# Attention into a weighted network on one core: the low words of the weights placed by GpSimd, halved first pieces, the means in two small products, and a new table of first steps

## The chip, the cores and the metric

One core of a Trainium2 chip runs one program. The metric is device time in microseconds, the median of several runs, from outside the program; a profiled execution also gives the span from the first to the last instruction. The engines are TensorE (PE; its weight loads are PEld), VectorE (DVE), ScalarE (ACT), GpSimd (POOL) and SyncE (SP), whose queue issues nearly all transfers. Each works through its own queue in order, and waits on semaphores for the others.

## The reference, cut to what matters

```
# q, k, v: (4, 8, 768, 64);  w1, w2: (512, 1024);  w3: (1024, 1024);  w_out: (1024, 512)
k_sum = k.reshape(B, H, 24, 32, D).max(axis=3)
v_sum = v.reshape(B, H, 24, 32, D).mean(axis=3)
scores_l = scale * q @ k.T            # only |i - j| < 16 counts
scores_s = scale * q @ k_sum.T + log(32)
a = softmax(concat(masked scores_l, scores_s))
x = a @ concat(v, v_sum)              # then (B * S, H * D) = (3072, 512)
out = ((x @ w1) * (x @ w2)) @ w3 @ w_out
```

`w1`, `w2`, `w3` and `w_out` come as 64-bit floats, as everything else comes as 32-bit floats.

## The kernel before, in words

**Units.** The 3072 tokens are worked in 6 units of 512 tokens. A unit has 4 pairs of heads, and each pair is a step of attention: 16 score products (`sc`), then VectorE's masked minimum (`reduce`) and ScalarE's exponentials (`expose`), GpSimd's small addition on the sums (`invert`, tile `mx`), VectorE's reciprocal, a normalization, 16 transposes (`tp`), two copies out of PSUM (`evacuate`, tile `pt`), 16 products with the values (`po`), and `keep_x`, which keeps x as two words whose sum is exact (a high and a low one). When the 4 pairs of a unit are there, `gate` makes 8 slices f of `(x @ w1) * (x @ w2)`, 24 products each, and `project` multiplies by the folded matrix `wp` and stores.

**Fold.** `w3 @ w_out` is made once, in `fold_weights`: 32 pairs (i, j), each of three products 128x512 (high by high, low by high, high by low). Slices i = 0 and 1 accumulate in PSUM under the tag `mm`, slices 2 and 3 under the tag `tp`, of which there are two banks; the transposes and the `po` of attention use those same two banks. When a slice is complete, `store` copies it to `wp` (ScalarE the high word, VectorE the low one), and frees its bank.

**Weights.** Each 64-bit weight is two 32-bit words. A piece of 512 columns (512 KB) is loaded into a buffer `wraw` of a ring of 10. `convert` turns it into two 32-bit words for TensorE: ScalarE's Prelu rescales the upper words into `wf`; VectorE shifts `wf` left by 3 (line 175) and joins the top 3 bits of the lower words (line 178); ScalarE rounds `wf` to the high word of `w` (line 188); VectorE subtracts for the low word (line 109). In the listings a number after `w` or `wp` tells tiles apart; the first weights are, in order, w_106 and w_115 (w_93 and w_102 after the change) for slices 0 of `w_out` and `w3`; w_253 (w_283) and w_357 (w_385) are slices 2 and 3 of `w_out`, and w_415 (w_448) slice 4 of `w3`.

**Means.** `v_sum` of the first batch is made by TensorE: 6 products of a matrix of constants (`mean_sb`) with rows of v. Those of other batches, and all `k_sum`, are VectorE's reductions.

**Order.** SP's and TensorE's queues are in the order in which the program writes them; the other engines' are put in order by a scheduler. The first part runs in steps t, one for each piece of weights that is worked. `EARLY` is the order of the first pieces, `EARLY_PRODUCTS` that of the fold; `FIRST[s]` is the step in which the scores of pair s are begun, for the first 8 pairs; `LOADS` and `WORK` say which other loads and works go with which piece or step; `RATE` and `LATER_RATE` say how many columns of products TensorE is given in a step; `NORMALIZE` and `SECOND` choose the engine that normalizes a pair, and that makes its second copy out of PSUM. From pair 8 on, two pairs are worked at a time (the last loop of the program), and GpSimd normalizes.

Of the kernel before, what the change touches and what calls it, by code (L numbers as in the profile page):

```python
# [19 lines left out]
P = 128  # L20
# [10 lines left out]
FIRST = (15, 18, 20, 22, 27, 32, 37, 44)  # L31
# [4 lines left out]
    *(("wo", 0, 0), ("w3", 0, 0), ("wo", 0, 1), ("w3", 1, 0), ("wo", 1), ("w3", 2, 0), ("w3", 3, 0)),  # L36
    *(("w3", 0, 1), ("w3", 1, 1), ("wo", 2), ("w3", 2, 1), ("w3", 3, 1), ("wo", 3)),
# [10 lines left out]
NORMALIZE = "VAAAAAAA"  # L48
SECOND = "AAAVAVVA"
SOONER = 400  # L50
RING = 10
# [19 lines left out]
def attention_moe(ctx, tc, qG, kW, kT, vP, vW, vB, mask, w1, w2, w3T, wo, out):  # L71
# [24 lines left out]
    make_identity(nc, ident)  # L96
    mask_sb = const.tile([P, 3, KR], F32, name="mask_sb")


    mean_sb = sb.tile([P, S // P, P], F32, name="mean_sb", tag="v", bufs=2)  # L100
    nc.gpsimd.memset(mean_sb, 0.0)
    for i in range(P // BLOCK):
        for at in (CUT, CUT - 64):
            part = mean_sb.rearrange("p t n -> p (t n)")[i * BLOCK : (i + 1) * BLOCK, at + i :: P + P // BLOCK]
            nc.gpsimd.memset(part[:, : S // P], 1.0 / BLOCK)
# [22 lines left out]
    def weight(name, i, src, shape, part=None):  # L128

        n = src.shape[1] // 2  # L130
        parts = range(n // PIECE) if part is None else [part]
        units.append((name, i, shape, list(parts), len(todo) + len(parts) - 1))
        for k in parts:
            todo.append(src[:, 2 * k * PIECE : 2 * (k + 1) * PIECE])

    def start_loads(at_least):

        while todo or due_loads:
# [8 lines left out]
            nc.sync.dma_start(raw, todo.pop(0))  # L147
# [4 lines left out]
    def convert(name, i, shape, parts, last):  # L152


        n = len(parts) * PIECE
# [6 lines left out]
        for k in range(len(parts)):  # L162
# [3 lines left out]
            low_words.append(words[:, :, 0])  # L166
            nc.scalar.activation(  # L167
                f[:, k * PIECE : (k + 1) * PIECE],
                words[:, :, 1].bitcast(F32),
                AF.Prelu,  # L170
                scale=2.0**-112,
                alpha=-(2.0**32),
            )
            yield
        nc.vector.tensor_scalar(out=bits, in0=bits, scalar1=3, scalar2=None, op0=ALU.logical_shift_left)  # L175
        for k, low_word in enumerate(low_words):
            some = bits[:, k * PIECE : (k + 1) * PIECE]
            nc.vector.scalar_tensor_tensor(  # L178
                out=some, in0=low_word, scalar=29, in1=some, op0=ALU.logical_shift_right, op1=ALU.bitwise_or
            )  # L180
            working.pop(0)
# [4 lines left out]
        at = parts[0] * PIECE  # L186
# [4 lines left out]
        have.update((name, i, part) for part in parts)  # L191

    def fold_weights(order):
        acc = {}
        for i, j in order:
            while not {("w3", i, j * P // PIECE), ("wo", j // 2, j % 2 * DO // PIECE)} <= have:
                yield 0
# [58 lines left out]

    def mean_products(tiles):
        po = ps.tile([P, 512], F32, name="means", tag="sc", bufs=4)
        for i in range(S // P):
            nc.tensor.matmul(  # L260
                po[:KR, :DM],
                lhsT=mean_sb[:, i, :KR],
                rhs=tiles[i // 2][:, i % 2],
                start=i == 0,
                stop=i == S // P - 1,
            )
        return po
# [90 lines left out]
    def normalize_alone(s, sm, mx):  # L358

        if NORMALIZE[s] == "A":  # L360
            for j in range(NI):
                nc.scalar.activation(sm[:, j], sm[:, j], AF.Copy, scale=mx[:, 2, j : j + 1])
        else:
            nc.vector.tensor_tensor(sm, sm, mx[:, 2].unsqueeze(2).broadcast_to([P, NI, KR]), ALU.mult)

    def transposes(sm):

        tp = [ps.tile([P, 512], F32, name="tp", bufs=2) for _ in range(2)]
# [43 lines left out]
    def gate(f, x, hs):  # L412
        acc = []
        for w in range(2):
# [6 lines left out]
            for c in range(NC):  # L421
                while (GATES[w], k, c * FQ // PIECE) not in have:
                    yield 0
# [45 lines left out]
    def queue(name, i, part=None):  # L469
        src, shape = {"wo": (wo, (2, DO)), "w3": (w3T, (NJ, P)), "w1": (w1, (NC, FQ)), "w2": (w2, (NC, FQ))}[name]  # L470
        weight(name, i, src[i], shape, part)
# [118 lines left out]
    def means():  # L590
        po = mean_products(vraws)
        vraws.clear()
        vs[0] = sb.tile([KR, DM], F32, name="vs0", tag="pt", bufs=6)
        nc.scalar.copy(vs[0], po[:KR, :DM])

    LOADS = {
        7: [lambda: nc.sync.dma_start(mask_sb, mask)],
        8: [lambda: rows(1)],
        11: [lambda: fetch(0)],
        12: [lambda: keys(1)],  # L600
        13: [lambda: keys(0)],
        14: [lambda: rows(0)],
        15: [lambda: rows(2), lambda: fetch_values(0)],
        16: [lambda: fetch(1)],
        18: [lambda: keys(3)],
        21: [lambda: fetch(2), lambda: fetch_values(1)],
        22: [lambda: keys(2)],
        24: [lambda: fetch(3)],
        25: [lambda: fetch_values(2)],
        28: [lambda: fetch_values(3)],  # L610
# [3 lines left out]
        14: [means, lambda: summaries(0, 1, kraws.pop(1)), lambda: fill(1)],  # L614
        19: [lambda: fetch_sums(0)],
        20: [lambda: load_second(0), lambda: load_second(3), lambda: summaries(0, 2, kraws.pop(2)), lambda: fill(2)],
        21: [lambda: load_second(1), lambda: summaries(0, 3, kraws.pop(3)), lambda: fill(3), lambda: fetch_sums(1)],
# [159 lines left out]
```

## Time and profile before

| what | value |
| --- | --- |
| time, median of 3 runs | 543.22 us (542.31 to 544.02) |
| the profiled execution: time; its span | 541.49 us; 539.7 us |
| mean granted TensorE clock | 0.993 |
| PE busy; PEld busy | 517.6 us (96%); 419.9 us (78%) |
| DVE; ACT; POOL busy | 238.6 us; 239.8 us; 56.8 us |
| read from HBM; written | 58.51 MB; 6.29 MB |

A line of a timeline gives the start and the length in us of a row of like instructions, engine, line, operation and tiles, the shapes, and how many; in brackets the idle time of the engine ahead of them and what ended it. A line of windows gives for a stretch its length, then the busy time of PE, PEld, DVE, ACT and POOL with numbers of instructions, the granted clock, the busy share of the transfer engines, and GB/s. A line of groups ends with busy time, mean ns of one, and idle time ahead. Matmuls of 32-bit words that aren't rounded are recorded as two.

### The profile page before, as it was taken

The page shows a single profiled execution, that of the slowest core. Times are in us where ns is not written, and L with a number is a line of the kernel's source. Part 1 is how long each engine was busy: PE and PEld are TensorE (multiplying, and loading weights), DVE is VectorE, ACT ScalarE, POOL GpSimd, SP SyncE. Part 2 cuts the span into 40 slices and gives each one's busy share as a digit, 9 for nine tenths or more (in the row PEclk, how much of TensorE's full clock was granted, in tenths as well). Part 3 has the DMA queues.
Part 4 walks back from the last instruction along what each step waited for, and adds up shares of the span by engine and source line. Part 5 has one row for each costly group of instructions (what it writes and reads, how often), then busy time and mean ns, then how long its engine had stood idle before and what let it go on. Part 6 is the DMA issues. An engine that isn't in the chain of part 4 may idle for free.

```text
span 539.7 us, 9919 instructions
## 1 busy us (share of the span) xinstructions
PE 517.6 (96%) x3852; PEld 419.9 (78%) x3852; DVE 238.6 (44%) x686; ACT 239.8 (44%) x688; POOL 56.8 (11%) x103
## 2 busy tenths in 40 slices
PE   2897999999999999999999999999999999899997
PEld 1655777888788888888888888888888888788885
DVE  5879889998504227633253043251142350222210
ACT  5548998876436127126254153261172361222210
POOL 1010221110003001103002011021020020000000
PEclk9997999999999999999999999999999999999999
DMA  8999699775614005642050150050150020000001
GB/s 305 406 371 342 193 306 350 244 210 169 205 57 152 0 24 146 202 142 80 0 149 21 60 170 21 0 166 23 60 170 1 16 60 39 21 21 0 1 19 58
DMA packets 30574, 67.21 MB, mean 125 GB/s; under 512 B 4032, under 2 KB 7616, under 8 KB 30528
## 3 DMA queue, kind: packets, MB, share of 16 engines
q1 hardware_dynamic: 27072, 60.30, 34.7%
q10 hardware_dynamic: 3456, 6.29, 3.1%
q8 instruction: 30, 0.49, 0.4%
q14 instruction: 16, 0.13, 0.1%
HBM read 58.51 MB, written 6.29 MB: 120 GB/s over the span
## 4 chain that ended last, share of the span: by engine, by line
PE 91%; DVE 3%; ACT 3%; DMA 1%; issue 1%; POOL 0%; SPq 0%; POOLq 0%; ACTq 0%
PE mm L113 79%; PE po L393 5%; PE sc L319 4%; PE tp L373 3%; DVE w L109 1%; DMA wraw<-in_w3T_dram 1%; DVE wf L178 1%; ACT w L188 1%; PE means L260 1%; ACT sm L347 1%; DVE wf L175 1%; ACT wf L167 0%; ACT pt L378 0%; ACT wp L211 0%; DVE wp L109 0%
## 5 line engine op out<-in xcount | busy, mean ns | idle before, releaser
L113 PE MATMUL mm<-x,w 128*128 128x512 f32 x1152 | 265.1, 390 | 0.0
L113 PEld LDWEIGHTS mm<-x,w 128*128 128x128 f32 x1152 | 215.4, 188 | 45.8 <-issue 0.5
L113 PE MATMUL mm<-wp,h 128*128 128x512 f32 x576 | 134.1, 391 | 0.0
L113 PEld LDWEIGHTS mm<-wp,h 128*128 128x128 f32 x576 | 107.5, 188 | 22.8 <-issue 0.2
L347 ACT ACTIVATE sm<-sm,mx 128x120 f32<-128x120 f32 x192 | 73.7, 386 | 17.4 <-DVE mx L333 16.4
L438 DVE TENSOR_TENSOR g<-mm,g 128x512 f32<-128x512 f32 x48 | 33.1, 690 | 93.2 <-PE mm L113 90.8
L439 ACT CAST h<-g 128x512 fp32r<-128x512 f32 x48 | 29.6, 617 | 90.4 <-DVE g L438 90.4
L113 PE MATMUL mm<-w,w 128*128 128x512 f32 x192 | 52.4, 424 | 12.4 <-ACT w L188 11.4
L113 PEld LDWEIGHTS mm<-w,w 128*128 128x128 f32 x192 | 37.0, 200 | 24.9 <-ACT w L188 13.3
L457 ACT COPY o<-mm 128x512 f32<-128x512 f32 x24 | 14.0, 584 | 81.4 <-PE mm L113 81.4
L382 DVE COPY pt<-tp 120x512 f32<-120x512 f32 x19 | 13.1, 690 | 75.6 <-PE tp L373 75.6
L109 DVE TENSOR_TENSOR h<-g,h 128x512 fp32r<-128x512 f32 x48 | 35.7, 744 | 24.1 <-ACT h L439 23.9
L435 ACT COPY g<-mm 128x512 f32<-128x512 f32 x48 | 28.0, 584 | 35.9 <-PE mm L113 35.9
L333 DVE CUSTOM_DVE_ANT_0 sm<-sc,mask_sb 128x120 f32<-128x120 f32 x192 | 40.9, 275 | 3.9 <-PE sc L319 3.9
L347 ACT ACTIVATION_READ_ACCUMULATOR sm<-sm,mx 128x1 f32 x192 | 36.4, 189 | 0.0
L306 POOL COPY k<-ks 128x96 f32<-128x96 f32 (+1 forms) x32 | 10.2, 331 | 248.1 <-DMA k<-in_kW_dram 207.4
L109 DVE TENSOR_TENSOR x<-po,x 128x512 fp32r<-128x512 f32 x24 | 16.6, 690 | 36.0 <-ACT x L404 36.0
L356 POOL TENSOR_TENSOR sm<-sm,mx 128x960 f32<-128x960 f32 x16 | 29.1, 1820 | 6.0 <-DVE mx L353 5.0
L167 ACT ACTIVATE wf<-wraw 128x512 f32<-128x512 f32 x40 | 26.2, 673 | 6.3 <-DMA wraw<-in_wo_dram 2.8
L393 PEld LDWEIGHTS po<-pt,v 120*64 120x64 f32 x768 | 23.7, 138 | 5.1 <-issue 2.5
L378 ACT COPY pt<-tp 120x512 f32<-120x512 f32 x24 | 14.0, 583 | 30.7 <-PE tp L373 30.7
L188 ACT CAST w<-wf 128x1024 fp32r<-128x1024 f32 (+1 forms) x25 | 21.9, 877 | 12.7 <-DVE wf L178 12.6
(33 smaller groups left out, 295.1 us busy)
## 6 DMA issues: line engine op xcount, KB each, us to landing
k<-in_kW_dram SPq DMA_DIRECT2D x24, 368.0 KB
wraw<-in_w3T_dram SPq DMA_DIRECT2D x16, 512.0 KB
wraw<-in_w_dram SPq DMA_DIRECT2D x16, 512.0 KB
q<-in_qG_dram SPq DMA_DIRECT2D x24, 256.0 KB
raw<-in_kT_dram SPq DMA_DIRECT2D x16, 384.0 KB
out_dram<-o ACTq DMA_DIRECT2D x24, 256.0 KB
v<-in_vW_dram SPq DMA_DIRECT2D x24, 192.0 KB
raw<-in_vB_dram SPq DMA_DIRECT2D x12, 384.0 KB
```

The costliest lines, as they stand in the source:

```text
L109: eng.tensor_tensor(dst, src, hi.bitcast(F32), ALU.subtract)
L113: nc.tensor.matmul(acc, lhsT=a, rhs=b, start=first and i == 0, stop=last and i == len(terms) - 1)
L167: nc.scalar.activation(f[:, k * PIECE : (k + 1) * PIECE], words[:, :, 1].bitcast(F32), AF.Prelu, scale=2.0**-112, alpha=-(2.0**32),)
L188: nc.scalar.copy(hi, f)
L319: nc.tensor.matmul(sc[h][64 * g : 64 * g + 64, i * KR : (i + 1) * KR], lhsT=q[rows, i * P + 64 * g : i * P + 64 * g + 64], rhs=k[rows, i, ...
L333: nc.vector.tensor_tensor_reduce(out=sm[:, j], in0=sc[h][:, i * KR : (i + 1) * KR], in1=mask_sb[:, 0 if blk == 0 else 2 if blk == BLOCKS - ...
L347: nc.scalar.activation(sm[:, j], sm[:, j], AF.Exp, bias=mx[:, 0, j : j + 1], scale=-1.0, accum_out=mx[:, 1, j : j + 1])
L356: nc.gpsimd.tensor_tensor(sm, sm, mx[:, 2].unsqueeze(2).broadcast_to([P, NI, KR]), ALU.mult)
L393: nc.tensor.matmul(po[cols, at : at + 64], lhsT=v[:, g, i, cols], rhs=pt[g][:, (h * NBLK + i) * 64 : (h * NBLK + i + 1) * 64], start=True, ...
L435: nc.scalar.copy(g, a[:, :U])
L438: nc.vector.tensor_tensor(g, acc[1][:, :U], g, ALU.mult)
L439: nc.scalar.copy(h[:, 0], g)
```

## The change

GpSimd takes the lower words of a piece in its `wraw` buffer, multiplies them by 2^-29 and clips at 7, which leaves their top 3 bits as a number; VectorE then shifts `wf` and joins both in one operation, where it took two. The first four pieces have 256 columns (slice 0 of `w_out` and of `w3`, by halves). The means are made with 24 columns: 24 products of 24x128, of which four write side by side in 32 partitions each, four copies out of PSUM, 4 products that spread the result over the wanted rows, and one copy; GpSimd makes the two matrices of constants in step 3 (`CONSTANTS`), the second by 8 copies of the identity. Normalization of pairs 1, 3 and 5 goes from ScalarE to VectorE (that of pair 0 was there), the second copies of pairs 3, 5 and 6 go from VectorE to ScalarE, and that of pair 4 from ScalarE to VectorE. The steps and the tables are new. In the last loop, when nothing is left to begin, the second pair's transposes use two banks of the tag `sc`.

```
-FIRST = (15, 18, 20, 22, 27, 32, 37, 44)
+FIRST = (18, 20, 22, 25, 31, 38, 42, 45)
...
-    *(("wo", 0, 0), ("w3", 0, 0), ("wo", 0, 1), ("w3", 1, 0), ("wo", 1), ("w3", 2, 0), ("w3", 3, 0)),
-    *(("w3", 0, 1), ("w3", 1, 1), ("wo", 2), ("w3", 2, 1), ("w3", 3, 1), ("wo", 3)),
+    *(("wo", 0, 0, 256), ("w3", 0, 0, 256), ("wo", 0, 256, 256), ("w3", 0, 256, 256), ("wo", 0, 512)),
+    *(("w3", 1, 0), ("wo", 1), ("w3", 2, 0), ("w3", 3, 0), ("w3", 0, 512), ("w3", 1, 512), ("wo", 2)),
+    *(("w3", 2, 512), ("w3", 3, 512), ("wo", 3)),
...
-NORMALIZE = "VAAAAAAA"
-SECOND = "AAAVAVVA"
+NORMALIZE = "VVAVAVAA"
+SECOND = "AAAAVAAA"
...
+            nc.gpsimd.tensor_scalar(
+                out=words[:, :, 0], in0=words[:, :, 0], scalar1=2.0**-29, scalar2=7.0, op0=ALU.mult, op1=ALU.min
+            )
             yield
-        nc.vector.tensor_scalar(out=bits, in0=bits, scalar1=3, scalar2=None, op0=ALU.logical_shift_left)
-        for k, low_word in enumerate(low_words):
-            some = bits[:, k * PIECE : (k + 1) * PIECE]
+        for (k, length), low_word in zip(parts, low_words):
+            some = bits[:, k - at : k - at + length]
             nc.vector.scalar_tensor_tensor(
-                out=some, in0=low_word, scalar=29, in1=some, op0=ALU.logical_shift_right, op1=ALU.bitwise_or
+                out=some, in0=some, scalar=3, in1=low_word, op0=ALU.logical_shift_left, op1=ALU.bitwise_or
             )
...
     def mean_products(tiles):
         po = ps.tile([P, 512], F32, name="means", tag="sc", bufs=4)
         for i in range(S // P):
-            nc.tensor.matmul(
-                po[:KR, :DM],
-                lhsT=mean_sb[:, i, :KR],
-                rhs=tiles[i // 2][:, i % 2],
...
+            for p in range(NPAIR):
+                nc.tensor.matmul(
+                    po[32 * p : 32 * p + NB, :P],
+                    lhsT=constants["means"][:, i],
+                    rhs=tiles[i // 2][:, i % 2, p * P : (p + 1) * P],
...
+        means = sb.tile([P, P], F32, name="means_sb", tag="pt", bufs=6)
+        nc.vector.memset(means, 0.0)
+        for p in range(NPAIR):
+            nc.scalar.copy(means[32 * p : 32 * p + NB], po[32 * p : 32 * p + NB, :P])
+        yield
+        po = ps.tile([P, 512], F32, name="means", tag="sc", bufs=4)
+        for p in range(NPAIR):
+            nc.tensor.matmul(po[:KR, p * P : (p + 1) * P], lhsT=constants["spread"][:, p, :KR], rhs=means, start=True, stop=True)
+        vs[0] = sb.tile([KR, DM], F32, name="vs0", tag="pt", bufs=6)
+        nc.scalar.copy(vs[0], po[:KR, :DM])
...
-        15: [lambda: rows(2), lambda: fetch_values(0)],
+        17: [lambda: rows(2)],
...
-    RATE = 6600
-    LATER_RATE = 6944
+    RATE = 5600
+    LATER_RATE = 8944
...
-                        pts.append(evacuate(transposes(sms.pop(last[k])[0])))
+                        spare = {} if now or k == 0 else {"tag": "sc", "bufs": 4}
+                        pts.append(evacuate(transposes(sms.pop(last[k])[0], **spare)))
```

How the order moves, in three places. In each listing a row is an instruction of one engine's queue (line, operation, tiles, shape), with a count where it stands several times.

At the start of ScalarE's queue: the Prelu of the first pieces and the casts to the high words. Before, with pieces of 512 columns:

```order
L167 ACTIVATE wf<-wraw 128x512 x2
L188 CAST w_106<-wf 128x512
L167 ACTIVATE wf<-wraw 128x512
L188 CAST w_115<-wf 128x512
L167 ACTIVATE wf<-wraw 128x512
L188 CAST w_106<-wf 128x512
```

The same start after the change:

```order
L163 ACTIVATE wf<-wraw 128x256 x4
L163 ACTIVATE wf<-wraw 128x512
L185 CAST w_93<-wf 128x256
L185 CAST w_102<-wf 128x256
L185 CAST w_93<-wf 128x256
L163 ACTIVATE wf<-wraw 128x512 x2
L185 CAST w_102<-wf 128x256
```

The first cast stood behind two pieces of 512 columns; it now stands behind four of 256 and one of 512.

In TensorE's queue, from the scores of pair 0 to the products `po` of pair 0 (w_357 and w_385 are the last slice of `w_out` in the fold's first part). Before:

```order
L319 MATMUL sc<-k,q 64x120 x16
L113 MATMUL mm<-w_357,w_115 128x512 x6
L113 MATMUL mm<-w_357,w_137 128x512 x6
L113 MATMUL mm<-w_357,w_171 128x512 x6
L113 MATMUL mm<-w_357,w_196 128x512 x6
L373 MATMUL tp<-ident,sm 120x64 x16
L319 MATMUL sc<-k,q 64x120 x16
L113 MATMUL mm<-w_106,w_415 128x512 x6
L113 MATMUL mm<-w_162,w_415 128x512 x6
L113 MATMUL mm<-w_253,w_415 128x512 x3
L393 MATMUL po<-pt,v 64x64 x16
```

And after:

```order
L347 MATMUL sc<-k,q 64x120 x16
L106 MATMUL mm<-w_385,w_102 128x512 x6
L106 MATMUL mm<-w_385,w_157 128x512 x6
L106 MATMUL mm<-w_385,w_196 128x512 x6
L106 MATMUL mm<-w_385,w_218 128x512 x6
L347 MATMUL sc<-k,q 64x120 x16
L106 MATMUL mm<-w_93,w_448 128x512 x6
L106 MATMUL mm<-w_185,w_448 128x512 x6
L402 MATMUL tp<-ident,sm 120x64 x16
L106 MATMUL mm<-w_283,w_448 128x512 x6
L106 MATMUL mm<-w_385,w_448 128x512 x6
L422 MATMUL po<-pt,v 64x64 x16
```

The transposes of pair 0 stood right behind the fold's first part; now the scores of pair 1 and 12 products of slice 4 stand between.

In GpSimd's queue, from the first means to the first additions on `mx`. Before:

```order
L306 COPY k<-ks 128x4x24
L294 COPY v<-vs_314 24x512 x4
L306 COPY k<-ks 128x4x24
L352 TENSOR_SCALAR mx<-mx 128x8 x2
L294 COPY v<-vs_314 24x512 x2
```

And after:

```order
L170 TENSOR_SCALAR wraw<-wraw 128x512 x5
L334 COPY k<-ks 128x4x24
L322 COPY v<-vs_367 24x512 x2
L170 TENSOR_SCALAR wraw<-wraw 128x512
L322 COPY v<-vs_367 24x512 x2
L170 TENSOR_SCALAR wraw<-wraw 128x512 x5
L380 TENSOR_SCALAR mx<-mx 128x8
L334 COPY k<-ks 128x4x24
L380 TENSOR_SCALAR mx<-mx 128x8
```

The addition on pair 0's `mx` stood behind copies alone; it now stands behind the lower words of five more pieces of weights.

More of the change, by code (lines that the diff above doesn't have):

```diff
@@ L126, in attention_moe, with weight @@
     begun, due_loads, kraws, vraws = [0], [], {}, {}
-    def weight(name, i, src, shape, part=None):
+    def weight(name, i, src, shape, at=None, length=PIECE):
         n = src.shape[1] // 2
[L131 to L134, printed above, removed]
+        parts = [(k, PIECE) for k in range(0, n, PIECE)] if at is None else [(at, length)]
+        units.append((name, i, shape, parts, len(todo) + len(parts) - 1))
+        for k, length in parts:
+            todo.append(src[:, 2 * k : 2 * (k + length)])
     def start_loads(at_least):
@@ L158, in convert @@
         low_words = []
-        for k in range(len(parts)):
+        for k, length in parts:
             raw = loading.pop(0)
@@ L190, in convert @@
         low(nc.vector, lo, f, hi)
-        have.update((name, i, part) for part in parts)
+        have.update((name, i, c) for c in range(at, at + n, P))
     def fold_weights(order):
@@ L195, in fold_weights @@
         for i, j in order:
-            while not {("w3", i, j * P // PIECE), ("wo", j // 2, j % 2 * DO // PIECE)} <= have:
+            while not {("w3", i, j * P), *(("wo", j // 2, j % 2 * DO + c) for c in range(0, DO, P))} <= have:
                 yield 0
@@ L421, in gate @@
             for c in range(NC):
[L422 removed]
+                while (GATES[w], k, c * FQ) not in have:
                     yield 0
```

128 lines of the change are left out of this document (70 added, 58 removed).

## The prediction

> **What bounds the kernel now.** I read the page's busy times first, then windows cut at the places where TensorE's work changes.
>
> ```profile
> span 539.7 us, 9919 instructions
> PE 517.6 (96%) x3852; PEld 419.9 (78%) x3852; DVE 238.6 (44%) x686; ACT 239.8 (44%) x688; POOL 56.8 (11%) x103
> ```
>
> ```profile
> 0.00:9.50 9.50, 0.00 (x0) 0.00 (x0) 2.94 (x6) 4.33 (x6) 1.85 (x15) 1.00 0.77 263
> 9.50:17.75 8.25, 7.27 (x15) 3.79 (x15) 7.98 (x14) 6.03 (x10) 0.00 (x0) 1.00 1.03 404
> 17.75:28.44 10.69, 8.74 (x36) 6.59 (x36) 8.70 (x15) 5.54 (x9) 0.00 (x0) 1.00 1.02 405
> 28.44:45.57 17.13, 17.13 (x90) 11.50 (x90) 12.94 (x33) 10.38 (x29) 3.66 (x6) 1.00 1.04 379
> 45.57:52.55 6.98, 3.20 (x49) 2.59 (x49) 6.53 (x10) 5.37 (x9) 0.23 (x1) 0.64 1.04 325
> 52.55:87.00 34.45, 33.54 (x372) 26.26 (x368) 30.65 (x87) 30.76 (x97) 6.55 (x14) 0.97 0.84 273
> 87.00:463.70 376.70, 376.70 (x2909) 310.41 (x2905) 155.02 (x506) 162.50 (x506) 44.52 (x67) 1.00 0.32 100
> 463.70:468.60 4.90, 3.51 (x98) 3.20 (x97) 1.68 (x3) 1.75 (x3) 0.00 (x0) 1.00 0.01 3
> ```
>
> From 87 to 463.7 us TensorE, the first busy figure, is never idle. What can be won lies before 87, in the 1.4 us idle at 463.7 to 468.6, and in the means. Up to 45.57 the transfer engines are full (share 1.02 to 1.04, about 405 GB/s, so 1.29 us for a piece of 512 KB); VectorE, the third figure, is nearly full from 9.5 to 17.75 and from 45.57 to 87. The worst stretch is 45.57 to 52.55, where the granted clock is 0.64. TensorE's timeline:
>
> ```profile
> 28.44 3.95 PE L113 MATMUL mm<-w,w 128*128 128x512 f32 x16 [0.53 <-DVE w L109]
> 32.23 5.31 PE L260 MATMUL means<-rows,mean_sb 128*120 128x512 f32 x12
> 38.85 1.05 PE L319 MATMUL sc<-k,q 64*64 64x120 f32 x32
> 39.84 5.73 PE L113 MATMUL mm<-w,w 128*128 128x512 f32 x24
> 47.97 0.36 PE L373 MATMUL tp<-ident,sm 64*120 64x64 f32 x1 [2.41 <-DVE wp L109]
> 49.70 1.11 PE L373 MATMUL tp<-ident,sm 64*120 64x64 f32 x15 [1.37 <-DVE wp L109]
> 52.55 4.54 PE L113 MATMUL mm<-w,w 128*128 128x512 f32 x15
> ```
>
> A fold product costs 0.24 us (5.73 over 24). Pair 0's transposes wait twice for VectorE to free the `tp` banks, and the 15 products behind them run at 0.30 us each. What VectorE does meanwhile:
>
> ```profile
> 46.16 1.16 DVE L364 TENSOR_TENSOR sm<-sm,mx 128x960 f32<-128x960 f32 x1
> 47.83 1.22 DVE L109 TENSOR_TENSOR w<-wf,w 128x1024 fp32r<-128x1024 f32 x1
> 48.97 0.68 DVE L109 TENSOR_TENSOR wp<-mm,wp 128x512 fp32r<-128x512 f32 x1
> ```
>
> **The change part by part.** Prices by shape:
>
> ```profile
> L178 DVE SCALAR_TENSOR_TENSOR wf<-wraw,wf 128x512 uint32<-128x512 uint32 x40 | 26.6, 690 | 0.5
> L167 ACT ACTIVATE wf<-wraw 128x512 f32<-128x512 f32 x40 | 26.2, 673 | 6.3 <-DMA wraw<-in_wo_dram 2.8 <-DMA wraw<-in_w3T_dram 1.8 <-DMA wraw<-in_w_dram 1.5
> L188 ACT CAST w<-wf 128x1024 fp32r<-128x1024 f32 x15 | 15.7, 1050 | 5.9 <-DVE wf L178 5.7
> L175 DVE TENSOR_SCALAR wf<-wf 128x1024 uint32<-128x1024 uint32 x15 | 10.3, 689 | 0.4 <-ACT wf L167 0.4
> ```
>
> *Lower words.* VectorE loses one operation of 0.69 us for each 1024 columns. GpSimd gains one of 512 for each piece, beside ScalarE's Prelu (0.67). No row has that operation; GpSimd's nearest rows, and VectorE's beside them:
>
> ```profile
> 38.29 0.99 POOL L294 COPY v<-vs 24x512 f32<-24x512 f32 x1 [5.54 <-ACT vs L594]
> 39.32 0.61 POOL L294 COPY v<-vs 24x512 f32<-24x512 f32 x1
> 94.57 1.30 DVE L109 TENSOR_TENSOR w<-wf,w 128x1024 fp32r<-128x1024 f32 x1
> 94.85 1.28 POOL L294 COPY v<-vs 24x256 f32<-24x256 f32 x1
> 95.79 0.88 DVE L109 TENSOR_TENSOR h<-g,h 128x512 fp32r<-128x512 f32 x1
> 217.31 1.79 POOL L356 TENSOR_TENSOR sm<-sm,mx 128x960 f32<-128x960 f32 x1 [1.02 <-DVE vs L248]
> 217.80 1.84 DVE L109 TENSOR_TENSOR h<-g,h 128x512 fp32r<-128x512 f32 x1 [0.45 <-ACT h L439]
> ```
>
> A copy of 512 takes 0.61, and the operation with two inputs 1.79 for 960, so 0.95 for 512: the new one lies between, under the 1.29 in which a piece lands, and GpSimd keeps up. But the two engines hold each other. The copy at 94.85 ends behind VectorE's subtraction (95.87), and the next subtraction takes 0.88 where 0.69 is usual; the one at 217.80 waits for GpSimd's end and takes 1.84. So a lower word can cost VectorE nothing (it falls beside a reduction or an operation on PSUM), 0.4 (twice the 0.2 of a copy of 256), 0.62 (the 1.15 of the last row, by columns), or its whole 0.95. I take 0.3, that is 0.4 in three cases of four; the ends stay for the range.
>
> The Trainium skill (SBUF — State Buffer, section Who interferes with whom) says that a VectorE instruction with two SBUF inputs and a GpSimd instruction that reads SBUF exclude each other for a whole instruction, whoever comes first. By that rule the join and the low-word subtraction, which both have two, would wait out 0.61 to 0.95 wherever GpSimd is first, and the sum would be the second rival's. The trace agrees in kind (1.84 at 217.80), but has no row for the new operation.
>
> *First pieces.* The fifth load ends at the same number of bytes as the third did. ScalarE's first cast now stands behind that load's Prelu, and the first product needs three casts of 256, so it comes at about 9.8 instead of 9.5. That is hidden by the next wait, the second half of `w_out`'s slice 2. Loads are in order, and one landing is seen here:
>
> ```profile
> 13.56 0.70 ACT L167 ACTIVATE wf<-wraw 128x512 f32<-128x512 f32 x1 [0.30 <-DMA wraw<-in_w3T_dram]
> ```
>
> That is the 7th unit of 512 KB. The half slice stands at 13.35 units before (12 pieces, one of rows, the mask) and at 14.85 after (two key loads more): 21.7 and 13.5 + 7.85 x 1.29 = 23.6 us. Behind it come Prelu, join, cast and subtraction, 0.67 + 0.69 + 1.05 + 1.22 = 3.6: the products go on at 27.2, where VectorE's backlog held them until 28.44.
>
> *Means.* 12 half-rate records of 512 columns take 5.3 us; the 32 of 120 columns at 38.85 take 1.05, a third of what their columns would take in turn, so products in separate columns of the array do run side by side. I take 1.4 for the 24 and 0.9 for the four (bounds: 2.2 and 6.2 in all). But the third load of rows stands at 22.8 units (22.1 before): 13.5 + 15.8 x 1.29 = 33.9, while TensorE is there at 27.2 + 18 x 0.24 = 31.5. The last 8 products end at 34.4; the four copies wait behind the cast of w_385 and take about 1.5; then 0.9: 36.9, against 37.5. So 3 us less work brings 0.6.
>
> *The stretch at 45.57.* Its 6.98 us hold 1.7 of work at full clock (tp 0.68, sc 1.05), and the 15 slow products lose another 1.0: 6.3 lost. The first part of the fold now ends at 45.0; scores of pair 1 and 12 products (3.9) cover until 48.9. Pair 0's transposes want the normalization and slice 3's low word. ScalarE's exponentials stand behind the Prelu of the piece at 27 units, 28.4 + 8.4 x 1.38 (at 379 GB/s) = 40.0; with 8 exponentials, three casts to `wp`, one of w_448 and a Prelu between (3.1 + 1.7 + 1.1 + 1.3) they end at 47.2. GpSimd's addition also stands behind a piece at 31 units, 46 us. Then reciprocal 0.2, normalization 1.16, `wp` 0.68, with semaphores 50 to 51. I take 50.7 (ends 48.9 and 52): 1.8 of waiting, and 0.5 for w_448's low word. 6.3 - 2.3 = 4.0 won. From there to the gate the waits for ScalarE's copies (about 2, two with only 12 products ahead) are as long as the 0.9 idle and the smaller ones of before: 0, within 1.
>
> So the gate could begin 0.6 + 4.0 = 4.6 earlier, at 82.4. *Whether its weights are there* is VectorE's matter:
>
> ```profile
> 49.00:101.00 52.00, 50.38 (x479) 40.03 (x481) 47.68 (x126) 45.48 (x136) 9.32 (x20) 0.95 0.90 294
> 99.76 1.21 DVE L109 TENSOR_TENSOR w<-wf,w 128x1024 fp32r<-128x1024 f32 x1
> 102.44 0.74 PE L113 MATMUL mm<-x,w 128*128 128x512 f32 x2
> ```
>
> The second slice of w2 is ready at 101.0 and used at 102.4: nearly no slack, with VectorE 47.7 of 52 us busy since the end of w_415 (49.05). In the same stretch after: 8 shifts fall away (-5.5), three normalizations come (+3.5), a join, a second copy and some `wp` and gate work shift (-1.4): 44.3, plus 14 lower words at 0.3 = 4.2, plus half of the 4.3 idle: 50.7. From w_448's end at 46 that is 96.7. TensorE wants it at 82.4 + 60 x 0.23 = 96.2. Given back: 0.5, and as much again for ScalarE, nearly as busy (45.5): 1.0. Later weights stand further ahead of their use in the new order.
>
> *Tail.*
>
> ```profile
> 463.68 0.68 PE L373 MATMUL tp<-ident,sm 64*120 64x64 f32 x16
> 465.13 0.73 PE L373 MATMUL tp<-ident,sm 64*120 64x64 f32 x16 [0.76 <-ACT pt L378]
> 466.49 2.09 PE L393 MATMUL po<-pt,v 120*64 120x64 f32 x64 [0.62 <-ACT pt L378]
> ```
>
> With banks of their own the second transposes follow at once: 0.76 + 0.62, less 0.3 that the copies still need: 1.1.
>
> The sum: 4.6 - 1.0 + 1.1 = 4.7 off the profiled execution's 541.49 us (span 539.7 and 1.8 around it). That execution lies 1.7 under the median of 543.22; off the median it is 538.5.
>
> **The rivals.** *All of it shows*: lower words fall beside other work, pair 0 isn't late (1.8 less), the gate isn't either (1.0), and the small waits before it shrink by 1.5: 543.2 - 9.0 = 534.2. For it: VectorE is 4.3 us idle in that window; against: two engines there are over 87% busy.
>
> *GpSimd holds VectorE* (slower): each lower word costs 0.95. Then w2's slice is ready at 96.7 + 14 x 0.65 = 105.8, 9.6 late; 4.6 and 1.1 are won: 543.2 + 9.6 - 5.7 = 547.1. It decides from 0.62 a word on (101.2, 5.0 late, which with ScalarE's share eats the rest). For it: 1.84 at 217.80; against: 0.88 at 95.79.
>
> *The conversions take it all back*: VectorE's idle stays as it is and 0.45 a word is lost, or the four products of the means run in turn (3.9 more): 543, no change.
>
> **How the numbers follow.** About 0.3% (1.6 us) is what a measurement of this kernel can tell from no change. The forecast (536.5 to 541.5) gets 0.47, all of it showing 0.25, no change 0.15, slower 0.13. Faster is 0.47 + 0.25. The forecast's own range is 536.5 to 541.5; with the rivals, leaving a tenth out on each side, 533.5 to 544.8.
>
> **What would show it.** Right: no wait over 2.5 us on TensorE between 40 and 60, the clock at 1.0 there; the joins of VectorE at about 0.69 with few over 0.9; gate from 82 to 84; the two rows of transposes at the end without a gap. Wrong: joins with a mean over 0.95, GpSimd's new operation near 1 us and TensorE waiting on `w` behind the gate's start; a TensorE wait of over 4 us at the means.

## The result and the profile after

The changed kernel takes 565.38 us (median, 564.52 to 566.64) against 542.76 for the kernel before beside it: ratio 1.0415, interval 1.0391 to 1.044. It is 22.6 us slower where 4.7 us less were forecast, and far outside the range. The profiled execution has a span of 562.9 us. Its page, the line of busy times:

```profile
span 562.9 us, 10063 instructions
...
PE 521.7 (93%) x3896; PEld 422.5 (75%) x3896; DVE 232.0 (41%) x667; ACT 236.0 (42%) x674; POOL 152.2 (27%) x149
```

TensorE and VectorE work about as long as before; GpSimd has gone from 56.8 to 152.2 us. Two groups by shape (busy time, mean ns of one, then the idle time ahead of them and what ended it):

```profile
L170 POOL TENSOR_SCALAR wraw<-wraw 128x512 uint32<-128x512 uint32 x38 | 84.9, 2233 | 10.4 <-DMA wraw<-in_w_dram 6.5 <-DMA v<-in_vW_dram 1.3
...
L176 DVE SCALAR_TENSOR_TENSOR wf<-wf,wraw 128x512 uint32<-128x512 uint32 x38 | 26.7, 707 | 26.3 <-POOL wraw L170 25.8 <-DMA wraw<-in_w3T_dram 0.5
```

One lower word of 512 columns takes GpSimd 2.23 us, where the prediction had at most 0.95. The join on VectorE takes 0.71 us as forecast, but VectorE sat idle 25.8 us for GpSimd ahead of joins. The timelines of GpSimd and of VectorE show the queue:

```profile
14.54 21.18 POOL L170 TENSOR_SCALAR wraw<-wraw 128x512 uint32<-128x512 uint32 x9
36.66 12.31 POOL L170 TENSOR_SCALAR wraw<-wraw 128x512 uint32<-128x512 uint32 x5
```

```profile
21.69 0.69 DVE L176 SCALAR_TENSOR_TENSOR wf<-wf,wraw 128x512 uint32<-128x512 uint32 x1 [0.83 <-POOL wraw L170]
24.26 0.69 DVE L176 SCALAR_TENSOR_TENSOR wf<-wf,wraw 128x512 uint32<-128x512 uint32 x1 [1.88 <-POOL wraw L170]
26.82 0.69 DVE L176 SCALAR_TENSOR_TENSOR wf<-wf,wraw 128x512 uint32<-128x512 uint32 x1 [1.86 <-POOL wraw L170]
```

Nine words in a row without a gap, 21.18 / 9 = 2.35 us each. The joins follow at GpSimd's pace, 2.57 us from one to the next (24.26 - 21.69, 26.82 - 24.26), while a piece needs 1.29 us to land at the rate before the change. From 14.5 us on, GpSimd is a queue that falls behind. It holds up the loads too, since a buffer is free only when its join is done: SP's loads of weights (line 142) waited 15.9 us for joins in all, against 3.1 before (line 147). On TensorE:

```profile
11.76 1.65 PE L106 MATMUL mm<-w,w 128*128 128x512 f32 x3 [11.76 <-ACT w L185]
...
29.14 14.28 PE L106 MATMUL mm<-w,w 128*128 128x512 f32 x52 [4.41 <-DVE w L102]
43.35 1.51 PE L279 MATMUL means<-rows,picks 128*24 128x128 f32 x48
49.31 2.03 PE L293 MATMUL means<-means_sb,picks 128*120 128x128 f32 x8 [4.44 <-ACT means_sb L289]
...
69.97 0.36 PE L402 MATMUL tp<-ident,sm 64*120 64x64 f32 x1 [5.23 <-DVE sm L393]
...
103.35 0.34 PE L422 MATMUL po<-pt,v 120*64 120x64 f32 x4 [1.71 <-ACT pt L407]
...
104.80 2.79 PE L106 MATMUL mm<-x,w 128*128 128x512 f32 x11
```

Before, the row that begins with the fold's 15th record, as the one at 29.14 does here, was:

```profile
17.75 8.01 PE L113 MATMUL mm<-w,w 128*128 128x512 f32 x34 [0.37 <-DVE w L109]
```

The first product is at 11.76 instead of 9.52. The fold's 15th record is at 29.14 instead of 17.75; from there the 52 records up to the means run without a wait, and the means begin at 43.35 instead of 32.23. Their four last products wait 4.44, pair 0's transposes 5.23, and the gate begins at 104.80 instead of 87.00. That is 17.8 of the 23.2 us by which the span grew. The windows (after the length comes TensorE's busy time; the granted clock is third from the end) show the rest:

```profile
0.00:104.80 104.80, 71.70 (x600) 54.01 (x600) 64.16 (x146) 60.11 (x150) 82.10 (x72) 0.93 0.78 262
104.80:486.00 381.20, 377.00 (x2899) 308.32 (x2896) 154.10 (x502) 161.08 (x500) 70.10 (x78) 1.00 0.33 100
```

33 us of the first 104.8 are idle, at a mean clock of 0.93. Behind the gate 4.2 us are idle (381.20 - 377.00) where before had none. The tail came out as forecast, 32 transposes in one row and 0.20 of waiting where there were 0.76 and 0.62:

```profile
488.10 1.16 PE L402 MATMUL tp<-ident,sm 64*120 64x64 f32 x32
489.46 2.19 PE L422 MATMUL po<-pt,v 120*64 120x64 f32 x64 [0.20 <-ACT pt L407]
```

### The profile page after: what moved, and what is told of

The parts are those of the page before. It is cut to its first block, busy times and chain, and to the rows that moved or that the text cites. A ratio compares the mean times of both kernels' runs of the same rounds, so it can differ in the third digit from the quotient of the medians.

```text
span 562.9 us, 10063 instructions
## 1 busy us (share of the span) xinstructions
PE 521.7 (93%) x3896; PEld 422.5 (75%) x3896; DVE 232.0 (41%) x667; ACT 236.0 (42%) x674; POOL 152.2 (27%) x149
## 4 chain that ended last, share of the span: by engine, by line
PE 74%; POOL 4%; DMA 3%; DVE 3%; ACT 2%; issue 1%; POOLq 0%
PE mm L106 65%; PE po L422 3%; POOL wraw L170 3%; PE sc L347 3%; PE tp L402 2%; DMA raw<-in_kT_dram 2%; DMA wraw<-in_w_dram 2%; ACT sm L375 1%; DVE vs L244 1%; DVE w L102 1%; ACT sm L390 0%; POOL k L334 0%; DVE ks L227 0%; DVE h L102 0%; DVE wf L176 0%
## 5 line engine op out<-in xcount | busy, mean ns | idle before, releaser
L170 POOL TENSOR_SCALAR wraw<-wraw 128x512 uint32<-128x512 uint32 (+1 forms) x42 | 89.7, 2136 | 14.1 <-DMA wraw<-in_w_dram 6.5
L106 PE MATMUL mm<-w,w 128*128 128x512 f32 x192 | 56.2, 448 | 21.3 <-ACT w L185 12.6
L106 PEld LDWEIGHTS mm<-w,w 128*128 128x128 f32 x192 | 40.0, 216 | 34.0 <-ACT w L185 14.0
L334 POOL COPY k<-ks 128x96 f32<-128x96 f32 (+1 forms) x32 | 11.7, 379 | 194.8 <-DMA k<-in_kW_dram 186.4
L464 ACT COPY g<-mm 128x512 f32<-128x512 f32 x48 | 28.0, 584 | 33.9 <-PE mm L106 33.9
L411 DVE COPY pt<-tp 120x512 f32<-120x512 f32 x17 | 11.6, 690 | 74.1 <-PE tp L402 74.1
L176 DVE SCALAR_TENSOR_TENSOR wf<-wf,wraw 128x512 uint32<-128x512 uint32 (+1 forms) x42 | 28.4, 680 | 33.4 <-POOL wraw L170 32.9
L185 ACT CAST w<-wf 128x1024 fp32r<-128x1024 f32 (+2 forms) x27 | 22.0, 824 | 28.6 <-DVE wf L176 28.5
L380 POOL TENSOR_SCALAR mx<-mx 128x8 f32<-128x8 f32 x24 | 6.2, 259 | 96.7 <-ACT sm L375 96.2
L163 ACT ACTIVATE wf<-wraw 128x512 f32<-128x512 f32 (+1 forms) x42 | 26.3, 645 | 11.2 <-DMA wraw<-in_wo_dram 5.5
L102 DVE TENSOR_TENSOR w<-wf,w 128x1024 fp32r<-128x1024 f32 (+2 forms) x27 | 28.1, 1046 | 6.5 <-ACT w L185 6.5
```

The lines of the kernel that those rows point to most:

```text
L102: eng.tensor_tensor(dst, src, hi.bitcast(F32), ALU.subtract)
L106: nc.tensor.matmul(acc, lhsT=a, rhs=b, start=first and i == 0, stop=last and i == len(terms) - 1)
L163: nc.scalar.activation(f[:, k : k + length], words[:, :, 1].bitcast(F32), AF.Prelu, scale=2.0**-112, alpha=-(2.0**32),)
L170: nc.gpsimd.tensor_scalar(out=words[:, :, 0], in0=words[:, :, 0], scalar1=2.0**-29, scalar2=7.0, op0=ALU.mult, op1=ALU.min)
L176: nc.vector.scalar_tensor_tensor(out=some, in0=some, scalar=3, in1=low_word, op0=ALU.logical_shift_left, op1=ALU.bitwise_or)
L185: nc.scalar.copy(hi, f)
```

## The experiments

Ratios are to the kernel before, run on the same chip; one per cent is 5.4 us. Four theories were to be told apart: GpSimd's operation is slow by itself; VectorE holds it (or is held); the new order and the other edits cost as well; VectorE's work ahead of the gate sets the time.

**The price of the operation (price).** GpSimd tries forms on a scratch tile behind the last attention step:

```
for t in (apart, together, apart as float32, together as float32):
    tensor_scalar(t, t, 2**-29, 7.0, mult, min)   # line 692
    tensor_scalar(t, t, 2**-29, mult)             # line 693
    tensor_copy(t, t)                             # line 694
```

> The kernel before, with GpSimd trying operations of 128x512 on a scratch tile behind the last attention step, where VectorE is about 15% busy; three of each: two operations (mult, min), one (mult), a plain copy; on uint32 and on float32; with words 8 bytes apart and side by side. Theory 'the operation itself is slow': the uint32 operation with words 8 bytes apart takes 1.9 to 2.1 us here too, as its shortest in the changed kernel (1.97), and some of the other forms are far shorter (a float copy 0.6). Rival 'VectorE holds it': with VectorE nearly idle it takes 0.6 to 0.95.

Measured, GpSimd's groups by shape (mean ns of one at the end):

```profile
L692 POOL TENSOR_SCALAR trial<-trial 128x512 f32<-128x512 f32 x6 | 12.0, 2005 | 0.5
L692 POOL TENSOR_SCALAR trial<-trial 128x512 uint32<-128x512 uint32 x6 | 11.7, 1955 | 0.5
L693 POOL TENSOR_SCALAR trial<-trial 128x512 uint32<-128x512 uint32 x6 | 9.1, 1523 | 0.5
L693 POOL TENSOR_SCALAR trial<-trial 128x512 f32<-128x512 f32 x6 | 9.1, 1522 | 0.5
L694 POOL COPY trial<-trial 128x512 f32<-128x512 f32 x6 | 4.1, 682 | 0.4
L694 POOL COPY trial<-trial 128x512 uint32<-128x512 uint32 x6 | 3.7, 623 | 0.4
```

The operation takes 1.96 us beside a VectorE that is busy for 13.63 of the 53 us from 470 to 523. Neither the type nor the distance of the words matters: uint32 and float32 differ by 0.05 on average (one of the float32 words took 2.30), and one by one, words 8 bytes apart take 1.97 to 1.99 (that one apart, which ran beside a subtraction of VectorE), side by side 1.92 or 1.93. What counts is what is done to a word: nothing 0.62 to 0.68, one operation 1.52, two 1.96 to 2.01. So the copies that the prediction took as the lower bound say little of arithmetic. The theory holds; "VectorE holds it" is left with 0.27 of the 2.23. Only the profile of this kernel's one run (543.71 us) is used.

**The words taken back (words_back), alone (words_alone), every second one (words_half).**

```
- gpsimd.tensor_scalar(low, low, 2**-29, 7.0, mult, min)         # words_back
+ vector.tensor_scalar(bits, bits, 3, logical_shift_left)
- vector.scalar_tensor_tensor(some, some, 3, low, shift_left, or)
+ vector.scalar_tensor_tensor(some, low, 29, some, shift_right, or)
```

words_alone is the reverse of these lines in the kernel before; words_half has them for every second piece.

> The changed kernel with the lower words taken back from GpSimd: VectorE shifts the upper word and joins the lower one in two operations, as before; all else as changed. Theory 'GpSimd's 2.1 us a word is the whole loss': the rest of the change is worth what the prediction said or less, 536 to 543 us, the gate begins at 82 to 87 us, no wait of TensorE at the means over 2 us. Rival 'the new order costs as well' (loads of the second batch, means, first steps): over 548.

> The kernel before with the one edit alone: GpSimd places the lower words (40 pieces of 512), VectorE joins in one operation. Theory 'GpSimd's 2.1 us a word is the whole loss': 40 x 2.1 = 84 us of GpSimd's time ahead of the last weight, so the gate begins about 20 us late as in the changed kernel: 560 to 572 us. Rival 'the new order costs as well': 545 to 555.

> The changed kernel with every second piece's lower word on GpSimd, the other on VectorE in two operations. GpSimd then has 21 words x 2.1 = 44 us, one per two landed pieces (2.6 us and more). Theory 'GpSimd is slow but a queue that keeps up costs nothing': 537 to 544, within 3 us of the kernel with all words taken back. Rival 'a word on GpSimd is late by its 2.1 us each time, since VectorE's join waits for it': half of the loss stays, 548 to 556.

Measured: words_back 546.94 us, ratio 1.0098 (1.0071 to 1.0125); words_alone 562.19, 1.0375 (1.0355 to 1.0395); words_half 548.41, 1.0123 (1.0096 to 1.015). GpSimd's words alone cost 20 us in the old order and 17 in the new one. Half of them cost 1 to 2 us more than none, which the intervals cannot tell from nothing; VectorE still waited 11.6 us for GpSimd there. That is within the 3 us that the theory allowed, though the time lies in the rival's range (548 to 556), since words_back itself came out higher than expected. words_back lies between its theory (536 to 543) and its rival (over 548): with the lower words as before, the rest of the change loses 5 us. TensorE in it:

```profile
10.59 1.65 PE L106 MATMUL mm<-w,w 128*128 128x512 f32 x3 [10.59 <-ACT w L183]
...
32.02 3.98 PE L106 MATMUL mm<-w,w 128*128 128x512 f32 x16 [0.53 <-DVE w L102]
54.01 0.69 PE L400 MATMUL tp<-ident,sm 64*120 64x64 f32 x16 [2.16 <-DVE sm L391]
88.67 0.34 PE L420 MATMUL po<-pt,v 120*64 120x64 f32 x4 [2.99 <-ACT pt L405]
```

The gate begins at 90.85 instead of 87.00. So 3.9 of the 4.3 us by which this execution's span (544.0) is longer lie ahead of the gate; as the tail wins 1.1, some 1.5 more are lost behind it.

**One operation instead of two (one_op).**

```
- gpsimd.tensor_scalar(low, low, 2**-29, 7.0, mult, min)
+ gpsimd.tensor_scalar(low, low, 7.49 * 2**-32, mult)
```

> The changed kernel with GpSimd's operation cut to one multiplication by 7.49 x 2^-32, which rounds to 0 to 7 without the minimum (the lowest bits of the weights differ a little). Theory 'GpSimd's time per word is the loss': a word of 512 takes 1.52 instead of 1.95, so 42 words some 17 us less of GpSimd's time; the loss against the kernel with the words taken back (18 us) shrinks by more than half: 549 to 556 us. Rival 'it is the hand-over from GpSimd to VectorE, whatever its length': 560 or more.

Measured: 555.62 us, ratio 1.0257 (1.0239 to 1.0276).

```profile
L170 POOL TENSOR_SCALAR wraw<-wraw 128x512 uint32<-128x512 uint32 x38 | 66.4, 1747 | 12.3 <-DMA wraw<-in_w_dram 9.7 <-DMA wraw<-in_wo_dram 0.2
```

0.49 us less a word take 9 us off by ratio, half of the loss against words_back, just inside the theory's range. With words_half, where the hand-over stays for every second word and costs next to nothing, this says that the time follows GpSimd's time per word and not the hand-over.

**Lower words free (free_words) and absent (no_words).**

```
- gpsimd.tensor_scalar(low, low, 2**-29, 7.0, mult, min)         # free_words
- vector...(some, some, 3, low, shift_left, or)
+ vector...(some, some, 3, low, shift_left, and)
---
- vector...(some, low, 29, some, shift_right, or)                # no_words
```

> The changed kernel with GpSimd's operation left out: VectorE joins once, with the raw lower word and AND for OR, so that the weights are finite but not the right ones; loads, sizes and the number of VectorE's operations are the changed kernel's. It has what the prediction wanted of GpSimd, at no cost. Theory 'the new order loses some 5 us by itself, whatever VectorE has to do' (it was 5.1 slower with the words taken back): 543 to 548. Rival 'the prediction's other terms hold once the lower words cost nothing': 534 to 540.

> The kernel before without the lower words (VectorE only shifts; the weights lose their last three bits): 40 x 0.69 = 27.6 us of VectorE's work are gone, more than any way of placing the lower words could save. Theory 'VectorE's work sets the stretch from 45.57 to 87': 4 us and more less, 534 to 538. Rival 'the order of VectorE's and ScalarE's queues and the loads set it, not the amount of work': within 2 us, 539.5 to 542.

Measured: free_words 544.38 us, ratio 1.0039 (1.0023 to 1.0054); no_words 540.45, 0.9974 (0.9962 to 0.9986). These two show what the lower words could bring at most in these two orders of work, whose tables were left as they are. With VectorE's busy time down from 238.6 to 213.3 us the old kernel gains 1.4 us, as the rival said: with this order the amount of VectorE's work is not what the stretch waits for. In no_words pair 0's transposes still wait as long as before, 3.53 and 0.33 where it was 2.41 and 1.37:

```profile
48.02 0.27 PE L369 MATMUL tp<-ident,sm 64*120 64x64 f32 x1 [3.53 <-DVE wp L109]
48.62 0.78 PE L369 MATMUL tp<-ident,sm 64*120 64x64 f32 x15 [0.33 <-DVE wp L109]
...
85.31 14.14 PE L113 MATMUL mm<-x,w 128*128 128x512 f32 x60
```

And with GpSimd at no cost the change still loses 2.1 us, as the theory for free_words said. Its page and its TensorE:

```profile
PE 518.6 (95%) x3896; PEld 422.1 (78%) x3896; DVE 227.9 (42%) x667; ACT 237.1 (44%) x674; POOL 59.6 (11%) x107
```

```profile
37.51 0.85 PE L276 MATMUL means<-rows,picks 128*24 128x128 f32 x16 [2.57 <-DMA rows<-in_vP_dram]
39.71 2.03 PE L290 MATMUL means<-means_sb,picks 128*120 128x128 f32 x8 [1.35 <-ACT means_sb L286]
...
87.55 0.34 PE L419 MATMUL po<-pt,v 120*64 120x64 f32 x4 [2.87 <-ACT pt L404]
89.00 11.20 PE L106 MATMUL mm<-x,w 128*128 128x512 f32 x41
```

VectorE is busy 227.9 us with the same 667 instructions that take 232.0 in the changed kernel. So working side by side cost VectorE at most 4.1 us, 0.10 for each of the 42 words, and GpSimd 2.23 - 1.96 = 0.27 a word.

**The other edits one by one.** The tail and the means, each alone in the kernel before; the first pieces of 512 columns back (beside the words), and then the key loads behind again:

```
+ spare = {} if now or k == 0 else {"tag": "sc", "bufs": 4}    # tail_alone
+ transposes(..., **spare)
---
- 6 products 128*120 x 512                                      # means_alone
+ 24 products 128*24 x 128, 4 copies, 4 products 128*120 x 128
---
- ("wo", 0, 0, 256), ("w3", 0, 0, 256), ("wo", 0, 256, 256), ...  # back_long
+ ("wo", 0, 0), ("w3", 0, 0)
---
- LOADS 8: keys(0), rows(1); 9: keys(1); 10: mask                # keys_late
+ LOADS 7: mask; 8: rows(1); 12: keys(1); 13: keys(0)
```

> The kernel before with one edit: the last step's second transposes go to banks of the scores. Theory 'the waits at 465.13 and 466.49 end': 1.1 us less, that is 0.2%, 540.8 against 541.9; the profile shows both rows of transposes without a gap. Rival 'the copies are the bound there': the wait moves behind the transposes, 0 to 0.4 us less.

> The kernel before with one edit: the means as 24 + 4 products (2.6 us of TensorE as measured in the kernel with the words taken back, 1.51 + 1.10, against 5.31). Theory 'a wait on VectorE follows at 45.57 and takes it back': within 1 us of before, 541 to 543. Rival 'work taken off TensorE in front of the gate is won': 2.7 us less, 539.2.

> The changed kernel with the lower words taken back and first pieces of 512 columns again (all tables two steps earlier). Theory 'short first pieces cost the start' (first product at 10.59 where the kernel before has 9.50): first product at 9.5 and 1 to 3 us less than with the words taken back alone: 544 to 546 on this scale. Rival 'the start is hidden by later waits': 546 to 548.

> The changed kernel with the lower words taken back and first pieces of 512, and now the loads of the first two keys and the mask where the kernel before has them (behind, not ahead of, the third slice of w_out, which lands at 21.8 there and at 24.2 with the keys ahead). Theory 'the loads put ahead cost 1.4 us at 28.44 and a window of half clock': 542.5 to 545 on the scale where the order with the keys ahead has 546.5. Rival 'the later waits, for ScalarE's copies before the gate, take it back': 545.5 to 547.5.

Measured: tail_alone 540.46 us, ratio 0.9979 (0.9964 to 0.9994), 1.1 us less as forecast. It is the one version of the real computation here that beats both kernels. back_long 546.46, 1.0085 (1.0066 to 1.0104), against words_back's 1.0098: the short pieces put the first product at 10.59 (9.57 in back_long) and cost nothing that can be measured. keys_late 546.73, 1.0092 (1.0073 to 1.0111): the products go on at 28.32 (29.82 in back_long), as before the change, and the time does not move. The 1.5 us won there go to the third load of rows (2.06) and the copies of the means (2.47), and the copy before the gate is waited for as well (3.44), as the rival said:

```profile
35.34 1.07 PE L277 MATMUL means<-rows,picks 128*24 128x128 f32 x16 [2.06 <-DMA rows<-in_vP_dram]
38.88 2.03 PE L291 MATMUL means<-means_sb,picks 128*120 128x128 f32 x8 [2.47 <-ACT means_sb L287]
88.47 2.25 PE L420 MATMUL po<-pt,v 120*64 120x64 f32 x32 [3.44 <-ACT pt L405]
```

means_alone 548.92, 1.0121 (1.0101 to 1.0142): 2.7 us less work for TensorE makes the old kernel 6.6 us slower, outside both expectations. Its gate begins at 90.35 instead of 87.00, behind new waits for copies, and a wait for a transfer comes later:

```profile
87.89 0.34 PE L418 MATMUL po<-pt,v 120*64 120x64 f32 x4 [1.15 <-ACT pt L403]
89.38 1.04 PE L418 MATMUL po<-pt,v 120*64 120x64 f32 x28 [1.15 <-DVE pt L407]
...
130.71 1.00 PE L418 MATMUL po<-pt,v 120*64 120x64 f32 x16 [1.40 <-DMA v<-vs]
```

TensorE was not the bound at the means: with less work there it still waits as long at pair 0's transposes (3.53 and 0.33, where it was 2.41 and 1.37). The scheduler sets ScalarE's and VectorE's later work in another order, and that order's waits cost more. In the profiled execution (550.29 us, the slowest of the six) 5.1 of the 8.5 us more of span lie behind the gate: the wait of 1.40, and 3.7 us more of busy TensorE (451.43 against 447.77), where two pieces of 3.41 us ran at half clock. The trace shows these waits; that they follow from the order was not tried by itself, and the 6.6 us are not accounted for in full.

**The wait in the old order (store_first).** tail_alone, and:

```
+ with tc.high_priority(offset=SOONER):
      scalar.copy(wp[i][:, 0], done); low(vector, wp[i][:, 1], done, wp[i][:, 0])
```

> The kernel before with the tail edit and one more: the two stores of a folded slice (ScalarE's cast, VectorE's subtraction into wp) get priority, so that the fourth slice's subtraction stands ahead of pair 0's normalization instead of behind a weight's subtraction. Theory 'VectorE's order behind 45.57 makes the wait of 2.41 + 1.37 and the slow clock after it': 2 to 4 us less than with the tail edit alone (540.5): 536.5 to 538.5. Rival 'the normalization is the later of the two anyway': 539.5 to 541.5.

Measured: 543.39 us, ratio 1.0023 (1.0008 to 1.0037), by ratio 2.4 us slower than tail_alone, outside both expectations. The waits of 2.41 and 1.37 for the stores went as meant, and one of 2.90 for the normalization took their place, as the rival said; the gate begins at 86.82 (87.45 in tail_alone). But behind the gate there are now waits that tail_alone has not; that the stores' priority made them was not tried:

```profile
48.54 0.68 PE L374 MATMUL tp<-ident,sm 64*120 64x64 f32 x16 [2.90 <-DVE sm L365]
...
125.64 1.04 PE L394 MATMUL po<-pt,v 120*64 120x64 f32 x28 [0.73 <-POOL k L307]
...
132.51 7.76 PE L113 MATMUL mm<-x,w 128*128 128x512 f32 x33 [1.49 <-DVE g L439]
```

**The copy before the gate (copies_vector), the old means (means_old), both (both_old).** All in words_back:

```
- SECOND = "AAAAVAAA"
+ SECOND = "AAABVAAA"     # B: both copies of pair 3 on VectorE, with priority
```

> The changed kernel with the lower words taken back, and pair 3's two transposed copies done by VectorE, with priority, instead of by ScalarE, where they stand behind the Prelu of a piece that lands at 86.5 us. Theory 'the wait of 2.99 for that copy, just before the gate, and the window of half clock behind it are the order's loss': 2 to 4 us less than with ScalarE's copies (546.9), 543 to 545; the gate begins by 89.2 instead of 90.85. Rival 'the gate then waits for its weights': 546 to 548.

> The changed kernel with the lower words taken back and the means as the six products of 512 columns of the kernel before. Theory 'the short products only trade 2.7 us of TensorE for a wait of 1.3 for ScalarE's copies, and nothing waits for TensorE there': 545.5 to 548.5, the same as with the short ones (546.9). Rival 'the means edit itself loses, as it did alone (6.6 us)': 541 to 544.

> Both of these together: the changed kernel with the lower words taken back, the six old products, and pair 3's copies on VectorE. Theory 'the copies' place is the loss, the means are not': as with the copies on VectorE alone, 543 to 545. Rival 'the two losses add': 538 to 541.5.

Measured: copies_vector 547.02 us, ratio 1.0083 (1.006 to 1.0105); means_old 548.7, 1.0108 (1.0074 to 1.0143); both_old 545.27, 1.0054 (1.0036 to 1.0072). In copies_vector the copy's wait before the gate shrank from 2.99 to 1.40 and the gate began at 89.43 instead of 90.85, but the time hardly moved: the rival held, for TensorE then waited 0.25 and 0.76 for the gate's weights (0.36 in words_back). The old means make no difference that can be told (548.7, just above the theory's 548.5). Both together win about 0.4%, at the edge of the intervals: close to the theory's 543 to 545, though not for its reason, since the copies alone won nothing.

```profile
87.86 0.34 PE L423 MATMUL po<-pt,v 120*64 120x64 f32 x4 [1.40 <-DVE pt L406]
```

So of the 5 us about 2.4 go when pair 3's copies are VectorE's and the means are the old ones, and neither does it alone. Moving the loads ahead of the means won nothing (keys_late). Where the other half lies stays open.

## Why the prediction was wrong, point by point

*Lower words: the step that failed.* "A copy of 512 takes 0.61, and the operation with two inputs 1.79 for 960, so 0.95 for 512: the new one lies between ... and GpSimd keeps up." It lies far outside: 1.96 alone, 2.23 in the kernel. That is the term with the wrong size. No row of before had arithmetic of that size with a scalar on GpSimd, and neither bracket was of the same kind: one was a copy, the other a product of two tiles. With 2.23 against 1.29 a piece the queue grows. That is 17 us of the 22 (565.38 against 546.94, by ratio 4.15% against 0.98%). The Trainium skill (GPSIMD Engine Reference, section 3.1) gives 769 ns for 512 elements as a best case, by which GpSimd would keep up too (an estimate, 0.77 against 1.29). This instruction took 1.52 us with one operation and 1.96 with two.

The signs that were named for a failure are there in part: TensorE waits 4.44 at the means, and GpSimd's operation is far over 1 us; but the joins' mean is 0.71, not over 0.95, and behind the gate's start TensorE waits for `g`, `pt` and `x`, not for `w`.

*The lock: right in kind, too high.* 0.3 a word was taken, 0.10 measured for VectorE. The rival "GpSimd holds VectorE" had the sign, and 547.1, but not the mechanism: VectorE was not held, it waited for words that were not there. The Trainium skill (SBUF — State Buffer, section Who interferes with whom) speaks of whole instructions excluding each other. The traces agree in kind: VectorE's subtraction of 1024 takes 1.23 on average in free_words and 1.34 in the changed kernel, GpSimd's word 1.96 in price and 2.23. By one_op's slope (8.6 us for 0.49 a word) GpSimd's 0.27 would be some 5 of the 17 us, an estimate.

*VectorE's relief.* Some 5.5 us less of VectorE's work were counted so that the weights would be there for an earlier gate. no_words takes five times as much off and gains 1.4. "Nearly full" (47.7 of 52 us) was read as a bound; what TensorE waited for was one late piece, one copy or one normalization. The term of 1.0 for late weights stays untried, since no gate began at 82.4; with the gate at 89.00 free_words waits for none of them.

*First pieces.* The first product, forecast at 9.8, came at 9.81 in free_words, where the lower words cost nothing, and at 10.59 in words_back, where VectorE works them in two operations. That a later start is hidden held (back_long).

*The slice of w_out at 27.2.* In free_words it is 29.46. There ScalarE's Prelu waits for that piece until 25.68, where the landing was forecast at 23.6; the 3.8 us from there to the products are near the 3.6 forecast. So the landing was the term of the wrong size. In words_back it is 32.02, and there the cast behind the Prelu also waits 2.09 for VectorE.

*Means at 36.9 instead of 37.5.* TensorE's work was priced closely (1.4 + 0.9; at full clock 1.51 + 1.10 in words_back). But the rows that were forecast to land at 33.9 let TensorE go on only at 37.51 in free_words, after 2.57 of waiting; the wait for the copies (1.35) was near the 1.5 forecast, and the four products ended near 41.4.

*The stretch: the second step that failed.* It was to win 4.0, with 0, within 1, from there to the gate. Without GpSimd's cost pair 0's transposes ran at 55.02 with no wait, where 50.7 was forecast, since all before was late; and the copy before the gate was waited for 2.87, which the 0 did not hold. The gate began at 89.00, not 82.4; 4.3 of these 6.6 us were lost ahead of pair 0's transposes.

*Tail: right.* 1.1 forecast, 0.21% measured.

So without the wrong price the forecast would still have been wrong: free_words is 2.1 us slower than the kernel before, where 4.7 less were forecast. What makes up all of this second part stays open.

## What to carry to other kernels

Price an operation on an idle engine by a row of the same instruction, and where there is none, let the range reach to what makes that engine the bound: a copy (0.62) said nothing of arithmetic (1.52 and 1.96) on GpSimd. An engine that gets one piece of work per landed load must be faster than the loads; at 1.75 against 1.29 a piece, one_op still lost 8.6 us against words_back, while every second word (words_half) cost next to nothing. And a busy engine is not yet a bound: take the work away altogether first (no_words), and see what its absence is worth.

## What was unexpected of the hardware

GpSimd's time for 128x512 words: copy 0.62 to 0.68, one operation with a scalar 1.52, two 1.96 to 2.01 (all in price), whatever the type or a step of 8 bytes.

The clock falls on a grid. The windows cut by the granted clock, of the kernel before and of means_alone:

```profile
25.84:29.25 3.41, 1.54 (x6) 0.97 (x6) 2.27 (x4) 1.62 (x2) 0.00 (x0) 1.00 1.03 399
29.25:32.67 3.42, 3.42 (x16) 2.63 (x15) 2.73 (x6) 1.20 (x3) 0.51 (x1) 1.00 1.05 378
```

```profile
25.84:29.25 3.41, 1.53 (x6) 0.97 (x6) 2.26 (x4) 1.62 (x2) 0.00 (x0) 1.00 1.03 400
29.25:32.67 3.42, 3.42 (x10) 2.65 (x9) 2.74 (x6) 1.21 (x3) 0.58 (x1) 0.50 1.05 379
```

In both the same 1.9 us of 3.41 are idle, between the same products; the one keeps full speed, the other gets half for the next 3.42 us and takes 5.53 us for 16 products that take 3.95 in the kernel before. All half-speed pieces of these runs are 3.41 us long or a multiple, but for the last, which the end of the record cuts short; and the grid lies elsewhere in each execution. In means_alone a step of it, 25.84 to 29.25, holds all of the idle time. In the kernel before, counted back in steps of 3.41 from a half-speed piece that runs from 47.56 to 54.39, a step ends at 27.1, and the idle time is split into 1.3 and 0.6 us. The Trainium skill (TensorE: Matmul & The Clock Gate, section What's actually happening) says that the gate watches a free-running window of 3413 ns; the runs agree. For a kernel whose waits are 1 to 3 us long this adds or takes up to some 1.7 us a window (half of 3.41, an estimate) from one execution to the next, so one profile does not price a wait of that size: it takes rounds.
